# dh's product split between ScalarE and VectorE, with the orders of all stages laid anew

## The chip, the core and the metric

The kernel runs on one core of one Trainium2 chip. The time is device microseconds of one execution, from the core's own start to its end. Five engines run their own queues of instructions in order: TensorE (PE, with PEld for its weight loads), VectorE (DVE), ScalarE (ACT), GpSimd (POOL) and SyncE (SP, which here only issues transfers). An instruction that waits for a semaphore holds up everything behind it in its own queue, and nothing in the others unless they wait for its result.

## The reference

The forward pass is a layer norm, an S4 convolution of length L = 2048 over D = 512 channels with N = 128 states, and a gate from a two-layer network of width 1792. The kernel returns the forward output and the gradients of eleven inputs for a given `grad_out`:

```python
def _A_ref(u, A_re, A_im, B_re, B_im, C_re, C_im, log_dt, Dskip):
    ...
    P = jnp.exp(logdA[:, :, None] * l[None, None, :])
    K = jnp.einsum("dn,dnl,dn->dl", Cc, P, dB).real
    ...                                   # y = irfft(rfft(u padded) * rfft(K padded)), first L
    y = y + u * Dskip[None, None, :]
def _B_ref(x, w1, w2):
    h = jnp.einsum("bsd,df->bsf", x, w1)
    h = _silu(h)
    return jnp.einsum("bsf,fd->bsd", h, w2)
xn = _layernorm(x, axis=-1)
s = _A_ref(xn, ...)
g = _silu(_B_ref(xn, w1, w2))
return x + s * g
# reference(): this output, and jax.vjp(...)(grad_out) for u, A, B, C, log_dt, Dskip, w1, w2
```

All arrays are bf16. The term that the change touches belongs to the backward pass of the network: with DO the gradient at the output of w2, dh = (DO w2^T) * silu'(h), which then gives dw1 = xn^T dh and the part of dx that passes through w1.

## The kernel before

The work is in four stages, which by the trace take about 0 to 146 us (stage 1), 146 to 240 (stage 2), 240 to 399 (stage 3) and 399 to 668 (stage 5).

Stage 1 computes the network forward (ps_h, ps_o) beside the tables of powers for the convolution. The tables end in pairs of products XYg = ex * b_w and ex * b_s (L645), which are stored to DRAM (XYd) and come back in another layout as XYc (L840). Small masks that later stages use (mwk, MK, Sel, nSel, L315 to L345) are made on VectorE near the end.

Stage 2 turns these tables into the kernel K in chunks: ScalarE copies XYc into CY (L876, L877), VectorE multiplies (m, L891), TensorE sums (ps_k), and Kout goes to DRAM. Beside it xn is transposed (XT), goes through the first halves of a Fourier transform by matrix products (FA, FX), and w2 is transposed (w2o). When the last chunk of K is stored (Kud), it is loaded again as K_b, and its spectrum is made in stage 3, which holds the products of the spectra and the inverse transforms.

Stage 5 has two parts. Up to about 528 us come dw2 (ps_w of L1575, w for halves of one 128-row block), the "slabs" that collect the convolution's gradients per state (Gbd L1632, ps_V L1644, its eviction Vb, products T L1656 and L1659, ps_S L1674), YTl, and the first half of dh. From there come dx (ps_dx L1808, followed by the layer norm's backward on VectorE and ScalarE, L1813 to L1832), the rest of dh, dw1 (ps_w L1908, evicted into o10b), the last gradients of the states, and the output rows (zS, L1457 to L1470). dx needs W1 transposed, which seven transfers on SP bring (W1T, L1898, into the same memory KXW that dw2 used); they can start when dw2 is done.

dh is computed in 28 calls of `Bwd.dh(n)`: four chunks of 512 tokens by seven pairs of 128 rows. A call has ScalarE make sd = silu'(h) from hsb (L213), TensorE make eight matmuls into one PSUM tile ps_da (two such buffers, shared with ps_V), and VectorE multiply both into dhT (L1747). Then it issues on SP the load of an h to come and the stores that are pending, and calls `turn(n-1)`: eight transposes of the pair before into PSUM (pt_dh, L1762), an eviction into dhk (two buffers), and a store of dhk to dhd, which the next call issues.

What sets the order is not a scheduler but four strings. `play()` reads a string letter by letter; each letter advances one generator by one step, which issues its instructions on whichever engines it uses. A capital letter lets the step's evictions from PSUM (`ev`, L77) go by VectorE instead of ScalarE. In stage 5: h is one dh, w half a block of dw2, l a step of the slabs (49 in all), y a step of the states' YTl, u a load of w2's transpose, o one W1T load, x half of one dx tile, m one dw1 product, t one load of dh for dw1, f the states' end, z the output, r the rest.

Of the kernel before, what the change touches and what calls it, by code (L numbers as in the profile page):

```python
# [9 lines left out]
ALU = mybir.AluOpType  # L10
# [18 lines left out]
NU = 656  # L29


SCORE_1 = "pppppppppppgpgpgppGppgppppppggpppppgppgppppppppppgpppgpgppppppggppppppgpppppgppMpGGpppgppppgppgpppgpmpppppgppmgppgpppppppppgpgppppppmmmppgpgpmgpgGgttMmGmtmtgggmgGgmmmmgtgGGg"
SCORE_2 = (
    "guuuuuuuTutTKuWtttkkgkgttucgtggttttotguuuTgkttkTcktugtgtTgkottuuu",
    "uuuTTu",
    "tguuuwuwcttgtwUug",
    "uutKTtuggkuwkTTktuutKKKk",
)
SCORE_3 = (
    "TTU",  # L40
    "FFqkFFFfTfTftqqfqffqFFnDffnkffTkufffDfUfffdnudFUF",
    "aaadkadfdafdddfkDdFfafdfafBDvvvAkbnbvbdFadsgakdgaakigsbgdddGddDpaifDjjbiadjaaaxpbxbdevpivxBxvvtjzezxggpgsgstsgxzxzejxizeiztXzizbzqjbiyybsbpbcybsbgbpxssexjxpxpyzxsjxxxszexezczlylesssyszyslzZysZZCCCCCC",
)
SCORE_5 = (
    "uyuwuLLuWWhwyhuwyyLhlylwluyywlhllhllyluw",
    "whYYlwlLhYLwwwLlYyywLwlwlwWHyLlwwlwlLWywlyLylHwWyLllwylhwwolYhlLHlolYolhlolyloooHllLyLLxlhlx",
    "xzxxxxxhxzhhzxxhhxHfHxfxxxHxhxxHhtHthtxtxxzfxhxxMHxttxxttfzfmtffxttMMfftxmtfxtmxtfMtftrfmrffzMmrMfzzfffzzrm",
)


# [43 lines left out]
def drain(k, parts, names):  # L94

    for n in names:
        for _ in parts[n]:
            pass
# [10 lines left out]
def play(kk, score, **parts):  # L109

    for ch in score:
        if ch == " ":
            continue
        kk.by_dve = ch.isupper()
        next(parts[ch.lower()], None)
    kk.by_dve = False
# [95 lines left out]
def DSILU(nc, pool, out, in_):  # L212
    nc.scalar.activation(out=out, in_=in_, func=ACT.Derivative_silu)  # L213
# [531 lines left out]
def stage_1(k):  # L745
# [47 lines left out]
    def power():  # L793
        for _, _, fn, a in sorted(todo, key=lambda x: x[:2]):
            fn(*a)
            yield

    def tables():
        lo.close("bs", "tab", "pr")
        tables_open(k, fs)  # L800
        while True:
            tables_0(k)
            yield

    def forward():
        for _ in gf:
            yield
            settle(k)
    parts = dict(p=power(), m=gm, g=forward(), t=tables())
    i = SCORE_1.index("t")  # L810
    play(k, SCORE_1[:i], **parts)
    drain(k, parts, "pm")
    play(k, SCORE_1[i:], **parts)
    drain(k, parts, "g")
# [892 lines left out]
class Bwd:  # L1707
# [25 lines left out]
    def dh(self, n):  # L1733
        k, nc = self.k, self.k.nc
        tc_, f0 = n // 7, 2 * (n % 7)
        if f0 == 0:
            self.dhT = self.fb.tile([P, FT, 512], BF16, name="dhT", tag="dhT")
        assert k.w2t >= f0 // 2
        hs = self.hs.pop(n)
        sd = self.fw.tile([P, 2, 512], BF16, name="sd", tag="sd")  # L1740
        DSILU(nc, self.fw, sd[:], hs[:])
        ps = k.pd.tile([P, 2, 512], F32, name="ps_da", tag="pd")
        for j in range(2):
            ft = f0 + j
            for dk in range(DK):
                nc.tensor.matmul(out=ps[:, j], lhsT=self.W2T[:, ft // 2, dk, j * P:(j + 1) * P], rhs=self.DOT[tc_][:, dk], start=(dk == 0), stop=(dk == DK - 1))  # L1746
        nc.vector.tensor_tensor(out=self.dhT[:, f0:f0 + 2, :], in0=ps[:], in1=sd[:], op=ALU.mult)  # L1747
        if n + 3 < 28:
            self.ld_h(n + 3, nc.gpsimd if n < 7 else None)
        self.of[n] = self.dhT  # L1750
        self.flush()
        if n:
            self.turn(n - 1)
# [207 lines left out]
```

## Time and profile before

| | |
|---|---|
| median of 3 runs | 665.48 us (665.18 to 667.17) |
| profiled execution | 670.08 us |
| its span, first to last instruction | 668.1 us |
| granted TensorE clock, mean | 0.956 |
| busy: PE / DVE / ACT / POOL | 566.7 / 571.5 / 444.8 / 96.3 us |
| dh product on VectorE | 28 at 1221 ns |

In the profile's rows, a group is line, engine, operation, output and input, shapes and count; then busy time, the mean of one in ns, and after the last bar how long its engine had stood idle before such instructions, and for whom. A row of a stretch has the busy time and count of each engine, then the granted clock of TensorE, the share of the DMA engines that were busy, and GB/s. A row of the timeline has start, duration, engine and line, and in brackets the idle time ahead of it. SPq is the queue that issues transfers; its times are those of issuing, not of the transfer.

### The profile page before, as it was taken

To read this page: it belongs to the slowest core of one execution; us is meant where nothing else is said; L and a number is where in the kernel's file an instruction comes from. 1 tells how busy PE (TensorE), PEld (TensorE's weight loads), DVE (VectorE), ACT (ScalarE), POOL (GpSimd) and SP (SyncE) were. 2 spreads that over 40 slices of the span, in tenths; PEclk is the share of its full clock that TensorE was granted. 3 is DMA by queue.
4 is the path that set the end of the run, shared out by engine and by line. 5 is a ranking of instruction groups with operands and counts; after the bars stand their busy time and mean duration, and the time that the engine had idled before them with its cause. 6 is when DMAs were issued, how large, how long until landed. Compare 5 with 4: busy or idle time off the path is not lost. (4 is left out here: it accounts for less than half of the span.)

```text
span 668.1 us, 14321 instructions
## 1 busy us (share of the span) xinstructions
PE 566.7 (85%) x5668; PEld 341.6 (51%) x5668; DVE 571.5 (86%) x953; ACT 444.8 (67%) x538; POOL 96.3 (14%) x170
## 2 busy tenths in 40 slices
PE   2887897777686977799998779899999799999997
PEld 1333343245565766567775545454555344455553
DVE  7999899989799757998999998787888777889785
ACT  5799999967779725998989815763367345352232
POOL 1120100111002132121223152211111000000000
PEclk9999999898788797999999979999999799999999
DMA  8675777687699769965577889888969947986886
GB/s 257 215 256 183 261 257 262 232 288 209 180 281 318 228 181 269 306 225 168 152 231 211 179 236 248 254 241 198 234 189 207 267 126 215 270 249 218 276 278 199
DMA packets 173623, 154.58 MB, mean 231 GB/s; under 512 B 70575, under 2 KB 141751, under 8 KB 173557
## 3 DMA queue, kind: packets, MB, share of 16 engines
q1 hardware_dynamic: 157428, 112.70, 58.2%
q0 software_dynamic: 11920, 38.08, 18.2%
q10 hardware_dynamic: 4208, 2.89, 1.5%
q8 instruction: 44, 0.72, 0.4%
q14 instruction: 23, 0.18, 0.1%
HBM read 76.81 MB, written 67.65 MB: 216 GB/s over the span
## 5 line engine op out<-in xcount | busy, mean ns | idle before, releaser
L725 PE MATMUL ps_h<-XNT,W 128*128 128x512 bf16 x224 | 55.3, 392 | 18.7 <-ACT hs L77 14.5
L1746 PE MATMUL ps_da<-DOT,W2T 128*128 128x512 bf16 x224 | 53.2, 381 | 0.9 <-DVE dhT L1747 0.9
L698 PE MATMUL ps_o<-W,aT 128*128 128x512 bf16 x224 | 51.9, 379 | 2.0 <-ACT aT L727 2.0
L1808 PE MATMUL ps_dx<-KXW,dhT 128*128 128x512 bf16 x224 | 52.3, 387 | 0.0
L1575 PE MATMUL ps_w<-DO_all,KXW 128*128 128x512 bf16 x224 | 51.4, 379 | 0.0
L1908 PE MATMUL ps_w<-dhc,xn 128*128 128x448 bf16 x256 | 49.4, 352 | 0.0
L725 PEld LDWEIGHTS <-W 128*128 128x128 bf16 x224 | 22.3, 100 | 48.4 <-issue 25.2
L1747 DVE TENSOR_TENSOR dhT<-ps_da,sd 128x1024 bf16<-128x1024 f32 x28 | 34.2, 1221 | 13.5 <-ACT sd L213 11.2
L77 ACT CAST FA<-ps_f 128x1024 bf16<-128x1024 f32 x40 | 39.5, 1035 | 9.0 <-issue 6.2
L173 PE MATMUL ps_s<-FA,Wf 128*64 128x256 bf16 x384 | 36.9, 337 | 10.1 <-ACT FX L77 5.2
L77 ACT CAST FZ<-ps_i 128x1024 bf16<-128x1024 f32 x43 | 43.0, 1078 | 2.8 <-PE ps_i L187 2.8
L77 ACT COPY dhk<-pt_dh 128x1024 bf16<-128x1024 bf16 x18 | 18.2, 1009 | 30.0 <-PE pt_dh L1762 15.1
L1908 PEld LDWEIGHTS <-xn 128*128 128x128 bf16 x256 | 25.0, 98 | 23.7
L1817 ACT ACTIVATE dxn<-dxn,c,rstd 128x512 f32<-128x512 f32 x16 | 13.0, 814 | 35.6 <-DVE c L1816 35.6
L698 PEld LDWEIGHTS <-aT 128*128 128x128 bf16 x224 | 21.8, 98 | 28.7 <-ACT aT L727 2.5
L187 PEld LDWEIGHTS <-Vi 64*128 64x128 bf16 x576 | 27.4, 94 | 16.7 <-issue 6.2
L1808 PEld LDWEIGHTS <-dhT 128*128 128x128 bf16 x224 | 21.7, 99 | 25.3 <-issue 2.2
L1367 PE MATMUL ps_v<-FZ,TI 128*128 128x256 bf16 x192 | 26.2, 292 | 9.8 <-DVE FZ L162 8.7
L1746 PEld LDWEIGHTS <-W2T 128*128 128x128 bf16 x224 | 21.4, 98 | 25.5 <-issue 3.1
L173 PEld LDWEIGHTS <-Wf 128*64 128x64 bf16 x384 | 24.7, 124 | 18.1 <-issue 13.6
L727 ACT ACTIVATE aT<-ps_h 128x1024 bf16<-128x1024 f32 x28 | 31.5, 1130 | 3.1 <-PE ps_h L725 2.9
L1575 PEld LDWEIGHTS <-KXW 128*128 128x128 bf16 x224 | 20.8, 98 | 24.7 <-issue 2.3
(313 smaller groups left out, 1466.7 us busy)
## 6 DMA issues: line engine op xcount, KB each, us to landing
XTd<-XT SPq DMA_DIRECT2D x20, 512.0 KB, 7.0
XP<-UXd POOLq DMA_DIRECT2D x16, 512.0 KB, 5.3
XTl<-XTd SPq DMA_DIRECT2D x31, 256.0 KB, 3.7
hTd<-hs SPq DMA_DIRECT2D x28, 256.0 KB, 3.5
aTd<-aT SPq DMA_DIRECT2D x28, 256.0 KB, 3.2
dhc<-dhd SPq DMA_DIRECT2D x16, 448.0 KB, 5.9
XYd<-XYg SPq DMA_DIRECT2D x25, 256.0 KB, 3.4
hsb<-hTd SPq DMA_DIRECT2D x18, 256.0 KB, 3.7
```

The lines of the kernel that those rows point to most:

```text
L77: (k.nc.vector.tensor_copy if k.by_dve else k.nc.scalar.copy)(out=out, in_=in_)
L173: nc.tensor.matmul(out=ps[64 * h:64 * h + 64, c, j], lhsT=k.Wf[:, c, 0:64], rhs=A[:, 2 * (v + j) + h], start=True, stop=True)
L187: nc.tensor.matmul(out=ps[:, h, j], lhsT=Vc[z], rhs=y[z, c, v % 4 + j, :], start=(n == 0), stop=(n == len(Y) - 1))
L698: nc.tensor.matmul(out=pso[:], lhsT=aT[:, ft, tt * P:(tt + 1) * P], rhs=W2[:, ft, :], start=(ft == 0), stop=(ft == FT - 1))
L725: nc.tensor.matmul(out=ps[:, j], lhsT=W1[:, dk, ft * P:(ft + 1) * P], rhs=XNT[:, dk], start=(dk == 0), stop=(dk == DK - 1))
L727: nc.scalar.activation(out=aT[:, f0:f0 + 2, :], in_=ps[:], func=ACT.Silu)
L1367: k.nc.tensor.matmul(out=ps[:, j], lhsT=k.TI[:, t0 + j, c, :], rhs=Z[:, 2 * (t0 + j) + c], start=(c == 0), stop=(c == 1))
L1575: nc.tensor.matmul(out=ps[:], lhsT=A[:, t, :], rhs=k.DO[:, t, :], start=(t == 0), stop=(t == T - 1))
L1746: nc.tensor.matmul(out=ps[:, j], lhsT=self.W2T[:, ft // 2, dk, j * P:(j + 1) * P], rhs=self.DOT[tc_][:, dk], start=(dk == 0), stop=(dk == ...
L1747: nc.vector.tensor_tensor(out=self.dhT[:, f0:f0 + 2, :], in0=ps[:], in1=sd[:], op=ALU.mult)
L1808: nc.tensor.matmul(out=psx[:], lhsT=dhT[:, ft, t % 4 * P:(t % 4 + 1) * P], rhs=self.W1T[:, ft, :], start=(ft == 0), stop=(ft == FT - 1))
L1908: nc.tensor.matmul(out=ps[:], lhsT=k.xn[:, t, dk * P:(dk + 1) * P], rhs=ch[i][:, t, :], start=(t == 0), stop=(t == T - 1))
```

## The change

The product in `Bwd.dh` becomes two instructions. ScalarE copies ps_da from PSUM into its place in dhT, as bf16; VectorE then multiplies that place by sd in place, with both operands in SBUF.

```diff
             ft = f0 + j
             for dk in range(DK):
                 nc.tensor.matmul(out=ps[:, j], lhsT=self.W2T[:, ft // 2, dk, j * P:(j + 1) * P], rhs=self.DOT[tc_][:, dk], start=(dk == 0), stop=(dk == DK - 1))
-        nc.vector.tensor_tensor(out=self.dhT[:, f0:f0 + 2, :], in0=ps[:], in1=sd[:], op=ALU.mult)
+        d = self.dhT[:, f0:f0 + 2, :]
+        nc.scalar.copy(out=d, in_=ps[:])
+        nc.vector.tensor_tensor(out=d, in0=d, in1=sd[:], op=ALU.mult)
         if n + 3 < 28:
             self.ld_h(n + 3, nc.gpsimd if n < 7 else None)
```

All four strings are replaced as well. Their sequence is another, and so is the choice of capitals; in stage 5 the number of letters of each kind is the same. There, VectorE evicts 15 dhk of 28 (10 before), 9 YTl of 16 (6), 7 o10b of 16 (6), 5 blocks of dw2 of 14 (3) and 10 Vb of 32 (10). In stage 3 the capitals go from 39 to 38. The exponential that makes dtb4 stands between the first and the second string of stage 5; the first string is now 96 letters long (40 before), so it comes later. One line of the table, the second string of stage 5:

```diff
-    "whYYlwlLhYLwwwLlYyywLwlwlwWHyLlwwlwlLWywlyLylHwWyLllwylhwwolYhlLHlolYolhlolyloooHllLyLLxlhlx",
+    "LWwHwYllwlLolYlooohyLlLHooYollhlhl",
```

At the end of stage 1, on VectorE, the masks stood ahead of the last two pairs of XYg:

```order
L343 TENSOR_SCALAR mwk<-mwk 128x1
L344 TENSOR_SCALAR Sel<-mwk 128x32
L343 TENSOR_SCALAR mwk<-mwk 128x1
L344 TENSOR_SCALAR Sel<-mwk 128x32
L345 TENSOR_SCALAR nSel<-Sel 128x128
L645 TENSOR_TENSOR XYg<-ex,b_w 128x8x128
L645 TENSOR_TENSOR XYg<-ex,b_s 128x8x128
L645 TENSOR_TENSOR XYg<-ex,b_w 128x8x128
L645 TENSOR_TENSOR XYg<-ex,b_s 128x8x128
```

Now the last pair stands ahead of the masks from L327 on, and the pair before it further ahead still:

```order
L323 TENSOR_TENSOR mwk<-mwk 128x1
L324 SCALAR_TENSOR_TENSOR mwk<-mwk 128x1
L645 TENSOR_TENSOR XYg<-ex,b_w 128x8x128
L645 TENSOR_TENSOR XYg<-ex,b_s 128x8x128
L327 CAST mwk<-num 128x16
L328 TENSOR_SCALAR mwk<-mwk 128x16
L331 CAST MK<-mwk 128x16x2
L332 TENSOR_SCALAR MK<-mwk 128x16x2
L331 CAST MK<-mwk 128x16x2
```

The last four XYg have moved forward past the masks of L327 to L345.

Early in stage 2, on ScalarE, the second copy into CY (L876, L877) followed this work, where FA and FX belong to the spectrum of xn, XT to its transposes and Kout to the chunks of K:

```order
L546 COPY TF<-pt_tf 128x1024 x4
L77 CAST FA<-ps_f 128x4x64x4 x8
L77 COPY XT<-pt_xt 128x1024 x4
L77 CAST Kout<-ps_k 128x41x16 x2
L77 COPY XT<-pt_xt 128x1024 x2
L77 CAST FX<-ps_s 128x2x512
L876 COPY CY<-XYc 128x128x6
L877 COPY CY<-XYc 128x512x2
```

Now it comes behind one Kout and two XT, with a block of w2o between:

```order
L546 COPY TF<-pt_tf 128x1024 x4
L77 CAST FA<-ps_f 128x4x64x4 x8
L77 COPY XT<-pt_xt 128x1024
L77 COPY w2o<-pt_w_1799 128x1024
L77 CAST Kout<-ps_k 128x41x16
L77 COPY XT<-pt_xt 128x1024
L876 COPY CY<-XYc 128x128x6
L877 COPY CY<-XYc 128x512x2
```

Four XT, one Kout and one FX have moved behind the copy.

At the end of stage 5's first part, on SP, the W1T loads (DMA_TRANSPOSE) stood between loads for the slabs (XTl), loads of h (hsb) and stores of dhk; this is from the second of the seven on:

```order
L1898 DMA_TRANSPOSE KXW<-in_B_w_dram 128x2x512
L1621 DMA XTl_5911<-XTd 64x2048
L1898 DMA_TRANSPOSE KXW<-in_B_w_dram 128x2x512
L1731 DMA hsb<-hTd 128x1024
L1794 DMA dhd<-dhk 512x1x256
L1621 DMA XTl_5912<-XTd 64x2048
L1898 DMA_TRANSPOSE KXW<-in_B_w_dram 128x2x512
L1621 DMA XTl_5913<-XTd 64x2048
L1898 DMA_TRANSPOSE KXW<-in_B_w_dram 128x2x512 x3
L1731 DMA hsb<-hTd 128x1024
L1794 DMA dhd<-dhk 512x1x128 x2
L1731 DMA hsb<-hTd 128x1024
```

Now, from one row ahead of the first of the seven on:

```order
L1621 DMA XTl_5912<-XTd 64x2048
L1900 DMA_TRANSPOSE KXW<-in_B_w_dram 128x2x512
L1621 DMA XTl_5913<-XTd 64x2048
L1900 DMA_TRANSPOSE KXW<-in_B_w_dram 128x2x512 x3
L1731 DMA hsb<-hTd 128x1024
L1796 DMA dhd<-dhk 512x1x192
L1796 DMA dhd<-dhk 512x1x64
L1731 DMA hsb<-hTd 128x1024
L1796 DMA dhd<-dhk 512x1x256
L1900 DMA_TRANSPOSE KXW<-in_B_w_dram 128x2x512 x3
L1731 DMA hsb<-hTd 128x1024
L1796 DMA dhd<-dhk 512x1x128 x2
```

The last XTl load now stands between the first and the second transpose, and the other six transposes come in two groups of three.

Since the change adds two lines to `dh`, all lines behind it have numbers greater by two (L1898 is L1900, L1794 is L1796).

More of the change, by code (lines that the diff above doesn't have):

```diff
@@ L29 @@
 NU = 656
-SCORE_1 = "pppppppppppgpgpgppGppgppppppggpppppgppgppppppppppgpppgpgppppppggppppppgpppppgppMpGGpppgppppgppgpppgpmpppppgppmgppgpppppppppgpgppppppmmmppgpgpmgpgGgttMmGmtmtgggmgGgmmmmgtgGGg"
+SCORE_1 = "ppppppppppppgppggGpppppgppppggppppppgpppppggpppppppgpppppppppgggpppgppppgpppppGMppGpppgpppppgppppggppppppgpppgpmppppppppgpgppppppgmpmppgmpgpmpggmGMmmgtmtmmGggtmggGggtgmtGmGg"
 SCORE_2 = (
[L34 to L37, printed above, removed]
+    "ugTuuTuuuuuTtugTwKgktcTtggttkgttukuuouTtttkttcgt",
+    "gtgkktggkttTuouTuuuuuutugwuugtuUKtttcwgkuguugwukttkut",
+    "tTuWu",
+    "TtKkKk",
 )
 SCORE_3 = (
-    "TTU",
-    "FFqkFFFfTfTftqqfqffqFFnDffnkffTkufffDfUfffdnudFUF",
-    "aaadkadfdafdddfkDdFfafdfafBDvvvAkbnbvbdFadsgakdgaakigsbgdddGddDpaifDjjbiadjaaaxpbxbdevpivxBxvvtjzezxggpgsgstsgxzxzejxizeiztXzizbzqjbiyybsbpbcybsbgbpxssexjxpxpyzxsjxxxszexezczlylesssyszyslzZysZZCCCCCC",
+    "TT",
+    "UFFFFFffkfqqqtqtfffqFkftFFnfDnfkTffffDfffdkudUuFUF",
+    "aadaadadffdddnFnkdDffafaidffBDvbvAvbvaddgsbakgkaagbdFgdddsGdkdDpajjiDibadaabaxbiedxtvfvvppBvsxzjtgsxgsxziegpggxezxzxjzjzezzXbibtziijyybbspespbybcbbxxssxxppqgyzjxlxxxzsexcezjzsyeslysszzsssYzlyZZCCCCCC",
 )
 SCORE_5 = (
-    "uyuwuLLuWWhwyhuwyyLhlylwluyywlhllhllyluw",
-    "whYYlwlLhYLwwwLlYyywLwlwlwWHyLlwwlwlLWywlyLylHwWyLllwylhwwolYhlLHlolYolhlolyloooHllLyLLxlhlx",
-    "xzxxxxxhxzhhzxxhhxHfHxfxxxHxhxxHhtHthtxtxxzfxhxxMHxttxxttfzfmtffxttMMfftxmtfxtmxtfMtftrfmrffzMmrMfzzfffzzrm",
+    "uwuuuuWhWywLwyWyylYLhYwylywlwhwlwylllhuLlluHllYLWHyLylywlwllwylhWlllyHYwLwLwlwLwlLYHwYlLylwhlyLW",
+    "LWwHwYllwlLolYlooohyLlLHooYollhlhl",
+    "xzxxxxxxxzHxHzhxHxhxHffhxxxxxHhxxfHHttHtthxxxfzhxMxHxxftttxfftfftmMttxMtxxfftfxtxMMztmffMrtzMffzzfrrffmrtmmzz",
 )
```

## The prediction

> **What bounds the kernel now.** I read the page's first part for the engines, then the busy time by stretches for where each engine is full, then the groups of instructions for prices, and the timeline at the two places where the new orders differ most. The profiled execution took 670.08 us: its span is 668.1, so 1.98 lie around it, and it stands 4.6 above the median of 665.48. I sum against 670.08 and subtract the differences from the median.
>
> ```profile
> span 668.1 us, 14321 instructions
> PE 566.7 (85%) x5668; PEld 341.6 (51%) x5668; DVE 571.5 (86%) x953; ACT 444.8 (67%) x538; POOL 96.3 (14%) x170
> ...
> core 0: us, PE busy (x) PEld busy (x) DVE busy (x) ACT busy (x) POOL busy (x), PEclk, DMA share, GB/s
> ...
> 200.00:300.00 100.00, 79.68 (x1283) 62.67 (x1281) 81.47 (x114) 73.32 (x80) 24.36 (x47) 0.90 0.85 254
> 300.00:400.00 100.00, 85.39 (x1054) 64.47 (x1049) 96.07 (x80) 78.20 (x84) 27.49 (x42) 0.97 0.70 195
> 400.00:440.00 40.00, 36.40 (x355) 19.84 (x353) 33.28 (x56) 27.27 (x30) 8.89 (x15) 1.00 0.94 254
> 440.00:480.00 40.00, 38.84 (x383) 20.16 (x381) 31.80 (x49) 15.63 (x19) 8.37 (x15) 1.00 0.89 220
> 480.00:520.00 40.00, 38.69 (x449) 22.40 (x445) 34.66 (x52) 27.47 (x30) 5.56 (x11) 1.00 0.86 209
> ...
> 600.00:640.00 40.00, 40.00 (x215) 20.19 (x214) 33.82 (x65) 11.64 (x22) 0.00 (x0) 1.00 0.79 267
> ```
>
> VectorE is full in stage 3 (96.07 of 100), but dh's product does not run there. It runs from 413 to 605, where TensorE is the fuller engine in every stretch: 36.40, 38.84 and 38.69 of 40, then 40.00. So what VectorE gives up there can return no more than the time in which TensorE stands still for it, and from 600 on there is none.
>
> **The split itself.** These are the groups of stage 5 that it touches:
>
> ```profile
> L1746 PE MATMUL ps_da<-DOT,W2T 128*128 128x512 bf16 x224 | 53.2, 381 | 0.9 <-DVE dhT L1747 0.9
> L1747 DVE TENSOR_TENSOR dhT<-ps_da,sd 128x1024 bf16<-128x1024 f32 x28 | 34.2, 1221 | 13.5 <-ACT sd L213 11.2 <-PE ps_da L1746 2.2
> L213 ACT ACTIVATE sd<-hsb 128x1024 bf16<-128x1024 bf16 x28 | 29.3, 1056 | 0.0
> L77 ACT CAST Vb<-ps_V 128x1024 bf16<-128x1024 f32 x22 | 22.2, 1014 | 11.0 <-PE ps_V L1644 5.7 <-issue 5.1
> L77 ACT COPY dhk<-pt_dh 128x1024 bf16<-128x1024 bf16 x18 | 18.2, 1009 | 30.0 <-PE pt_dh L1762 15.1 <-DMA dhd<-dhk 14.2 <-ACT sd L213 0.6
> L1762 PE MATMUL pt_dh<-ident_bfloat,dhT 128*128 128x128 bf16 x224 | 17.1, 219 | 0.7 <-DVE dhT L1747 0.6
> L77 DVE COPY dhk<-pt_dh 128x1024 bf16<-128x1024 bf16 x10 | 6.8, 683 | 3.0 <-DMA dhd<-dhk 3.0
> L1469 DVE TENSOR_TENSOR zS<-zS,zg 128x1024 bf16<-128x1024 bf16 x8 | 5.5, 684 | 4.1 <-DMA zg<-gd 4.1
> ```
>
> VectorE loses 28 products of 1.221 us that read PSUM and gets 28 all-bf16 ones. The nearest row is zS at 684 ns, the same size and types in SBUF: 28 x (1.221 - 0.684) = 15.0 us less. ScalarE gets 28 casts of PSUM to bf16 at 128x1024. The nearest is Vb at 1.014: 28.4 us more. One dh's chain from TensorE's last matmul to the finished dhT grows from 1.22 to 1.01 + 0.68 = 1.70, and crosses two queues. Nothing waits for that at once: the transposes of a pair are issued only after the next pair's eight matmuls (53.2 / 28 = 1.90 us).
>
> The new order spends half of the relief: in stage 5 eleven more evictions go by VectorE (five dhk, three YTl, two KXW, one o10b). At 0.683, the dhk row, that is 7.5 us, so VectorE keeps a net relief of 7.5 us over 265. For ScalarE the eight large ones return 8 x 1.009 = 8.1; with the three small ones, which I bound between 0 and the same 1.009 each, its net is +17 to +20 us. The stretch with the most ScalarE work in this stage, 480 to 520, has 27.47 of 40 and six products: 27.5 + 6.1 = 33.6. It stays off the bound, so I cost the casts at nothing; their cover is 12 us of ScalarE's idle time per 40, and without it each would cost up to 1.0.
>
> The page "VectorE: DVE Perf Modes" of the Trainium skill, section "Rules for kernel authors", speaks against this change: for an elementwise operation on a matmul's output it says to accept the slow rate, or to copy to SBUF first where many operations follow. Here one follows. By that rule the split only adds engine time, 28 x (1.01 + 0.68 - 1.22) = 13 us; the trace agrees on the sum, but those 13 us lie on an engine that idles.
>
> **Stages 1 and 2.** At the end of stage 1 the last two pairs of table products (XYg) move ahead of the masks of L327 to L345; in stage 2 the second CY copy moves forward in ScalarE's queue. The timeline of VectorE and then of ScalarE:
>
> ```profile
> 127.73 0.17 DVE L327 CAST mwk<-num 128x16 f32<-128x16 int32 x1
> ...
> 130.73 1.22 DVE L645 TENSOR_TENSOR XYg<-ex,b_w 128x1024 bf16<-128x1024 f32 x1
> ...
> 134.14 1.22 DVE L645 TENSOR_TENSOR XYg<-ex,b_s 128x1024 bf16<-128x1024 f32 x1
> ...
> 144.94 1.83 DVE L891 TENSOR_TENSOR m<-CY 128x1536 bf16<-128x1536 bf16 x2 [2.29 <-ACT CY L877]
> ```
>
> ```profile
> 130.32 1.13 ACT L631 ACTIVATE b_w<-b_w,halfpi 128x1024 f32<-128x1024 f32 x1
> ...
> 143.05 0.85 ACT L876 COPY CY<-XYc 128x768 bf16<-128x768 bf16 x1 [4.92 <-DMA XYc<-XYd]
> ```
>
> The masks fill 127.73 to 130.73, 3.0 us, ahead of the last four XYg. VectorE later stands 2.29 us for CY, which waits for the load of what these XYg store. Moving the masks behind them could bring the store 3.0 us forward, but the last XYg pair still needs b_w, ready at 131.45. It could then end at 131.45 + 2 x 1.14 = 133.7, not 135.4: at most 1.6. I take half, -0.75 (range 0 to -1.6).
>
> ```profile
> 168.53 0.71 ACT L77 CAST Kout<-ps_k 128x656 bf16<-128x656 f32 x1 [4.27 <-PE ps_k L945]
> ...
> 172.25 0.87 ACT L876 COPY CY<-XYc 128x768 bf16<-128x768 bf16 x1
> ```
>
> ```profile
> 174.17 2.70 DVE L891 TENSOR_TENSOR m<-CY 128x1536 bf16<-128x1536 bf16 x3 [4.50 <-ACT CY L877]
> ```
>
> ScalarE stood 4.27 us for the second Kout's matmuls with the CY copy queued behind, and VectorE 4.50 for CY. In the new order the copy comes after one Kout and two XT, not two Kout, six XT and an FX; five instructions and that wait no longer stand ahead, so the 4.50 can go whole. What is late next is the kernel's way from K to its spectrum, by the waits of 230 to 282 (total, count, longest):
>
> ```profile
> POOL K_b L997 <- DMA K_b<-Kud: 6.7, 1, 6.7
> ...
> ACT FA L77 <- issue: 6.2, 1, 6.2
> ```
>
> These waits between 230 and 282 follow the last K chunk, and their instructions are not shortened. What VectorE wins at 174 reaches the end only if the chunks come sooner. Between 0 and -4.5 I take -2. Stage 3 is VectorE's own: its evictions by VectorE go from 39 to 38 letters (one F and one Y more, two T and one Z fewer), the rest is the same work in another sequence: 0, range -2 to +2.
>
> **Stage 5 up to dx (399 to 528).** TensorE idles 3.60 + 1.16 + 1.31 = 6.1 us in the three stretches to 520, and most at the end, by the timeline:
>
> ```profile
> 519.17 6.16 SPq L1898 DMA_TRANSPOSE KXW<-in_B_w_dram  x3
> ...
> 522.16 0.69 DVE L77 COPY dhk<-pt_dh 128x1024 bf16<-128x1024 bf16 x1 [2.68 <-DMA dhd<-dhk]
> ...
> 523.84 0.78 PE L1644 MATMUL ps_V<-XTl,Gbd 128*32 128x256 bf16 x16 [3.09 <-DVE Gbd L1632]
> ...
> 527.91 3.17 PE L1808 MATMUL ps_dx<-KXW,dhT 128*128 128x512 bf16 x7
> ```
>
> In the chain that ended last, in order of time:
>
> ```profile
> 514.12 7.95 DMA dhd<-dhk
> ```
>
> And the stretches of 4 us, with the granted clock behind POOL's column:
>
> ```profile
> 520.00:524.00 4.00, 0.91 (x20) 0.61 (x16) 1.84 (x4) 3.03 (x4) 0.00 (x0) 1.00 1.20 258
> 524.00:528.00 4.00, 3.31 (x41) 1.59 (x38) 3.59 (x5) 0.00 (x0) 0.00 (x0) 0.58 1.09 246
> 528.00:532.00 4.00, 4.00 (x11) 1.44 (x12) 3.65 (x4) 0.00 (x0) 0.00 (x0) 0.57 0.99 268
> ```
>
> The dhk store issued at 514.12 took 7.95 us among the W1 transposes; VectorE stood for it, behind it Gbd, behind that TensorE: 3.09 + 0.69 idle in 520 to 528, and then 8 us at a granted clock of 0.57, worth 8 x 0.43 = 3.4. So the place costs about 7.2. The new order takes the XTl loads out from between the transposes and issues these as 1, 3 and 3. Two dhk stores stand between the two threes, and two after them. I think the stall gets smaller, because more dhk evictions leave VectorE's queue free for Gbd, but the store still goes out amid transposes. Between all of it gone (-7.2) and the slower case below (+8.4) I take -2; and of the 6.1 before it, where waits for VectorE are few, -0.5.
>
> The clock's recovery is a rule of "TensorE: Matmul & The Clock Gate", Part 1, of the Trainium skill: half rate after an idle window of some 3.4 us, full again after as long a busy one. By it the slow stretch would cost 3.4 x 0.5 = 1.7 and the place 5.5. The trace shows more than 8 us between 0.57 and 0.58, and I keep its 7.2.
>
> **Stage 5 from dx on.** TensorE is busy 40.00 of 40 at 600; a dh needs 1.90 + 17.1 / 28 = 2.51 us of it, ScalarE 1.06 + 1.01 and every other time 1.0 of dhk: 2.57 on average. Nearly even, so runs of four dh's could lag by under 1 us, which the dx between make up. I take 0, range -1 to +1.5; the last transfers, of the same kind and number, 0, range -1 to +1.
>
> **Sum.** -0.75 - 2 + 0 - 2.5 + 0 + 0 = -5.25: the profiled 670.08 becomes 664.8, and the median 660.2. I say 660.5.
>
> **Rivals.** (a) No net change, about 665.5: the 4.5 of stage 2 ends in the unchanged way from K, and stage 5 finds the same stall in another queue. For it speaks that TensorE leads all through stage 5; against it that two named stalls have their cause moved. (b) Larger gain, about 655: stage 2's 4.5, stage 1's 0.75 and most of the 7.2 (say 5.5) go, 10.75 in all. For it: VectorE's relief falls just where the chain ran over dhk and Gbd. Against: the dhk store's 7.95 is the DMA's. (c) Slower, about 671: the transposes as two threes. From the start of a three at 519.17 to dx at 527.91 went 8.74 us. After the last three the new order has four slab steps (about 0.85 each: 41.8 us of L1644 and L1674, over 49 letters) and two dh's, 8.4 us of TensorE work. If that work itself stands behind a dhk store caught among the transposes, TensorE idles 5 us more than now and the slow clock lasts 8 us longer: 5 + 3.4 = 8.4; less the 2.75 of stages 1 and 2, +5.65, or 671.1. It decides from where a dhk store issued behind the first three lands more than 8.4 us later. The rows behind the 41.8:
>
> ```profile
> L1644 PE MATMUL ps_V<-XTl,Gbd 128*32 128x256 bf16 x512 | 22.0, 290 | 5.6 <-DVE Gbd L1632 3.1 <-ACT Vb L77 1.8 <-DVE dhT L1747 0.6
> L1674 PE MATMUL ps_S<-T,Sel 128*32 128x512 bf16 x96 | 13.4, 394 | 1.9 <-DVE T L1659 1.0 <-DVE T L1656 0.7
> L1674 PE MATMUL ps_S<-T,nSel 128*32 128x512 bf16 x32 | 6.4, 395 | 0.0
> ```
>
> **Chances.** A measurement tells about 0.3%, 2.0 us, from no change. The forecast (657 to 663.4) 0.42, (b) 0.12: faster 0.54. (a) 0.14. (c) and other losses in orders that I could only read 0.32. The range 651 to 672 leaves out the far end of (b), under a tenth, and the far end of the losses, about a tenth. Those that win alone: 654 to 663.4.
>
> **What the profile after would show.** Right: the product at about 0.68, the casts near 1.01, VectorE's wait at the second CY under 1 us, TensorE's idle time before dx under 3.8, a shorter stretch at 0.57. Wrong: a TensorE wait of over 5 us just before ps_dx, ScalarE over 36 of 40 anywhere in stage 5 with TensorE waiting for dhT, or the span of stages 2 and 3 longer than now (146 to 399).

## The result: 1.6% slower, lost in stage 3

The changed kernel took 676.0 us (median of 4, 675.1 to 679.1) against 666.3 for the kernel before (median of 4, 665.2 to 667.2): a ratio of 1.0159, interval 1.0119 to 1.0198. Here and below, a ratio leaves out executions more than 1.5% above the fastest of their kernel. Its profiled execution took 675.44 us with a span of 673.6, 5.5 more than the 668.1 before. The profile of before is of an execution 3.8 above this median of 666.3, so the two profiles account for 5.5 of the 9.7 us between the medians; where the rest lies they do not show. The page's first part and the stretches of the changed kernel, with the columns as in the prediction:

```profile
span 673.6 us, 14323 instructions
PE 562.5 (84%) x5668; PEld 338.5 (50%) x5668; DVE 563.5 (84%) x962; ACT 462.8 (69%) x557; POOL 95.7 (14%) x170
...
200.00:300.00 100.00, 78.42 (x1305) 60.92 (x1304) 81.43 (x100) 76.38 (x84) 23.89 (x46) 0.97 0.82 245
300.00:400.00 100.00, 75.37 (x936) 56.33 (x935) 82.35 (x70) 72.43 (x78) 23.73 (x36) 0.90 0.73 171
...
440.00:480.00 40.00, 35.12 (x410) 20.36 (x408) 32.64 (x53) 26.78 (x30) 9.99 (x18) 0.98 1.09 217
480.00:520.00 40.00, 39.19 (x390) 20.67 (x389) 35.96 (x57) 21.46 (x26) 6.62 (x13) 0.98 0.96 240
```

One row stands out: 300 to 400, where VectorE had been busy 96.07 of 100 and is now busy 82.35. The stages can be cut at four marks, read from the first and last starts of a tile's instructions:

| mark | before | changed | difference of the piece |
|---|---|---|---|
| last group of ps_k (K is complete) | 238.8 | 231.7 | -7.1 |
| last group of ps_v (end of stage 3) | 398.7 | 405.4 | +13.8 |
| first ps_dx | 527.9 | 535.8 | +1.2 |
| end of the span | 668.1 | 673.6 | -2.4 |

So stages 1 and 2 won 7.1 us, stage 5 won 1.2, and stage 3 lost 13.8 (a piece is the time between two marks).

**Where stage 3 lost it.** The timeline of the changed kernel, VectorE and TensorE first:

```profile
384.09 1.23 DVE L125 TENSOR_TENSOR cm_t<-XP,KXW 128x2048 bf16<-128x2048 bf16 x1 [9.93 <-DMA XP<-DXd]
...
391.60 0.69 DVE L1434 TENSOR_TENSOR cG<-cG,co 128x1024 bf16<-128x1024 bf16 x1 [3.02 <-DMA cG<-in_grad_out_dram]
```

```profile
386.63 0.40 PE L187 MATMUL ps_i<-XP,Vi 64*128 64x256 bf16 x2 [10.12 <-DVE XP L126]
```

VectorE stood 9.93 us for a load of XP, then 3.02 for one of cG; TensorE stood behind it for 10.12. With another 0.80 for XP at 371.07, VectorE's waits for loads come to 13.75 us, the size of the loss. The XP loads are the last two from DXd, on POOL's queue, and beside them SP's queue brings the first inputs of dw2 by transposing loads (L1568, from aTd into KXW):

```profile
364.82 0.76 POOL L1425 DMA_DIRECT2D cG<-in_grad_out_dram  x1 [6.10 <-DVE cm_t L125]
365.57 1.09 POOL L1358 DMA_DIRECT2D XP<-DXd  x2
```

```profile
365.88 4.97 SPq L1568 DMA_TRANSPOSE KXW<-aTd  x1
372.46 1.27 SPq L91 DMA_DIRECT2D Sd<-S_s  x2
373.83 12.79 SPq L1568 DMA_TRANSPOSE KXW<-aTd  x1
```

```profile
L1358 POOL DMA_DIRECT2D XP<-DXd x8: 530/530/549, 301.7 to 366.1; - x8
...
DMA to landing us min/median/max: 3.6/4.8/17.9
```

Both XP loads stood behind the cG load, were issued together at 365.6 and 366.1, and 0.3 us after the first a transposing load was issued on SP. The first XP load landed in 5.4 us, the second in 17.9, and the co and cG loads behind it on POOL's queue took 18.1 and 17.1. Before, the two went out one by one, and none took over 6.9:

```profile
360.81 0.55 POOL L1358 DMA_DIRECT2D XP<-DXd  x1 [1.43 <-PE ps_i L187]
...
370.17 0.55 POOL L1358 DMA_DIRECT2D XP<-DXd  x1
```

```profile
363.76 3.06 SPq L1568 DMA_TRANSPOSE KXW<-aTd  x1
...
372.15 3.28 SPq L1568 DMA_TRANSPOSE KXW<-aTd  x1
```

```profile
DMA to landing us min/median/max: 3.8/4.9/6.9
```

While they ran together, the DMA engines were more than full by the sum of their packets' times (share, then GB/s, in the last two columns; the changed kernel):

```profile
366.00:372.00 6.00, 3.61 (x49) 2.93 (x48) 5.20 (x3) 4.57 (x6) 1.41 (x3) 1.00 0.99 209
372.00:378.00 6.00, 3.15 (x43) 2.17 (x40) 2.12 (x3) 4.22 (x5) 0.76 (x1) 1.00 1.30 99
378.00:384.00 6.00, 0.00 (x0) 0.00 (x0) 0.00 (x0) 0.00 (x0) 0.00 (x0) 0.59 1.42 131
```

From 372 to 378 they moved only 99 GB/s at a share of 1.30, and from 378 to 384 no engine computed at all. From the first transposing load on, the sequence of these loads and of the Sd stores on SP is the same in both kernels, and so is that of the cG and co loads on POOL. Only the place of the two XP loads among them moved.

### The profile page after: what moved, and what is told of

Same layout as the page of the kernel before. It is cut to its first block, busy times and chain, and to the rows that moved or that the text cites. A ratio compares the mean times of both kernels' runs of the same rounds, so it can differ in the third digit from the quotient of the medians.

```text
span 673.6 us, 14323 instructions
## 1 busy us (share of the span) xinstructions
PE 562.5 (84%) x5668; PEld 338.5 (50%) x5668; DVE 563.5 (84%) x962; ACT 462.8 (69%) x557; POOL 95.7 (14%) x170
## 5 line engine op out<-in xcount | busy, mean ns | idle before, releaser
L725 PE MATMUL ps_h<-XNT,W 128*128 128x512 bf16 x224 | 57.6, 405 | 15.8 <-ACT hs L77 10.2
L698 PE MATMUL ps_o<-W,aT 128*128 128x512 bf16 x224 | 54.1, 390 | 2.5 <-ACT aT L727 2.5
L1810 PE MATMUL ps_dx<-KXW,dhT 128*128 128x512 bf16 x224 | 50.5, 379 | 0.0
L187 PE MATMUL ps_i<-XP,Vi 64*128 64x256 bf16 x256 | 30.4, 279 | 17.5 <-DVE XP L126 13.7
L173 PE MATMUL ps_s<-FA,Wf 128*64 128x256 bf16 x384 | 34.9, 315 | 11.6 <-DVE FA L162 3.6
L1748 ACT CAST dhT<-ps_da 128x1024 bf16<-128x1024 f32 x28 | 28.2, 1006 | 9.2 <-PE ps_da L1746 8.9
L77 ACT COPY XT<-pt_xt 128x1024 bf16<-128x1024 bf16 (+1 forms) x31 | 28.1, 951 | 7.3 <-PE pt_xt L1019 6.0
```

The costliest lines, as they stand in the source:

```text
L77: (k.nc.vector.tensor_copy if k.by_dve else k.nc.scalar.copy)(out=out, in_=in_)
L173: nc.tensor.matmul(out=ps[64 * h:64 * h + 64, c, j], lhsT=k.Wf[:, c, 0:64], rhs=A[:, 2 * (v + j) + h], start=True, stop=True)
L187: nc.tensor.matmul(out=ps[:, h, j], lhsT=Vc[z], rhs=y[z, c, v % 4 + j, :], start=(n == 0), stop=(n == len(Y) - 1))
L698: nc.tensor.matmul(out=pso[:], lhsT=aT[:, ft, tt * P:(tt + 1) * P], rhs=W2[:, ft, :], start=(ft == 0), stop=(ft == FT - 1))
L725: nc.tensor.matmul(out=ps[:, j], lhsT=W1[:, dk, ft * P:(ft + 1) * P], rhs=XNT[:, dk], start=(dk == 0), stop=(dk == DK - 1))
L1748: nc.scalar.copy(out=d, in_=ps[:])
```

## The experiments

The theory after the result: the 10 us are a collision of the transposing load with the two XP loads, and without it the changed kernel is faster than before. A first rival: the XP loads are simply issued too late, behind cG. A second: the split itself costs, by ScalarE's queue. Letters of stage 3's last string: j is one XP load from DXd, y one piece of output with its next co and cG loads, l one transposing load for dw2; the diffs show only the part of the string that changes. Executions of one kernel spread over some 10 us on the chips of these runs (before: 664 to 676), so times are given as ratios to the kernel before on the same chip.

**Two transposing loads later.**

```diff
-yzjxlxxxzsexcezjzsyeslysszzsssYzlyZZCCCCCC"
+yzjxlxxxzsexcezjzsyesysszzsssYzlyZlZCCCCCC"
```

> The changed kernel, with two of the three early transposing loads for dw2 (L1568) moved one store of Sd later each in SP's queue at the end of stage 3. Theory (collision): in the changed kernel the last XP load (issued 366.1, landed 384.1) is slow because these transposing loads run through it; without them VectorE's wait of 9.93 us for XP falls under 1 us, the stage's end comes 8 to 13 us earlier, and the time is 663 to 668 instead of 676. Rival (late issue): the load is late because it stands behind a cG load in POOL's queue and two of them are issued together; then the wait stays near 10 us and the time at 674 to 677.

Ratio 0.9903 (0.9867 to 0.9939), or 0.994 by the medians of all executions (666.3 against 670.6); span 660.6, stage 3 ends at 392.9. The XP loads are issued at the same time as in the changed kernel, and as a pair, but now land in 4.4 and 6.6 us (no XP load of the kernel took over 7.4), and VectorE waits for none of them (POOL's and SP's timeline, and the XP tile's row):

```profile
366.24 1.09 POOL L1358 DMA_DIRECT2D XP<-DXd  x2
```

```profile
375.45 3.53 SPq L1568 DMA_TRANSPOSE KXW<-aTd  x1
```

```profile
DMA to landing us min/median/max: 3.8/4.8/7.4
```

That refutes the first rival: late issue alone costs nothing here.

**The two XP loads earlier.**

```diff
-ppqgyzjxlxxxzsexcezjzsyesl
+ppqjgjyzxlxxxzsexcezzsyesl
```

> The changed kernel, with the last two XP loads moved ahead of the last-but-one pair of cG and co loads in POOL's queue, transposing loads as they are. Both the collision theory and the late-issue rival expect the XP loads to be issued at about 357 to 362, ahead of the transposing load of 366, and the wait of 9.93 us to go: 663 to 668. They differ in what is left: by the collision, the co and cG loads, which still meet the transposing loads, stay slow (17 to 18 us to landing; VectorE's 3.0 us for cG stays); by late issue they land in about 4 us.

Ratio 0.9947 (0.9900 to 0.9994), span 662.9, stage 3 ends at 393.9. The loads go out at 358.5 and land in at most 7.2 us. The expectation about the rest missed: the cG and co loads that still meet the transposing loads of 366.5 and 374.4 land in 4.7 to 6.6 us, not in 17 to 18. So the transposing load does not slow every transfer that it meets.

**Which transposing load, and how many XP loads.** Three kernels, with one execution of each, so that their landing times say more than their spans: only the second transposing load later, only the third later, and only the first of the two XP loads earlier.

```diff
-zsyeslysszzsssYzlyZZCCCCCC"
+zsyesyslszzsssYzlyZZCCCCCC"     # second later
+zsyeslysszzsssYzyZZlCCCCCC"     # third later
-ppqgyzjxlxxxzsexcezjzsyesl
+ppqjgyzxlxxxzsexcezjzsyesl     # one XP load earlier
```

> The changed kernel with only the second of the three early transposing loads one store of Sd later, the third in its place. If it is the second one (issued 365.9, together with the two XP loads) that slows XP, VectorE's wait for XP is under 1.5 us and the span 660 to 664. If it takes the third one in the same stretch (issued 373.8), the wait stays over 5 us and the span over 667.

> The changed kernel with only the third of the three early transposing loads one store of Sd later; the second one still meets the two XP loads at about 366. If the second alone makes the collision: VectorE's wait for XP stays over 5 us, stage 3 ends after 400. If it takes the second and the third in one stretch: the wait is under 2 us and stage 3 ends at 393 to 396.

> The changed kernel with only the first of the last two XP loads moved ahead of the last-but-one cG and co pair in POOL's queue: the transposing load of 366 meets one XP load instead of two. If the pair is needed: the XP load lands in under 8 us and VectorE waits under 2 us for it, stage 3 ends at 393 to 397. If one is enough: it lands in over 12 us, the wait is over 4 us.

With the second one later the span is 663.3, stage 3 ends at 395.3, and XP lands in at most 6.8 us. With only the third later nothing is mended, span 675.7, stage 3 to 404.9, and one XP load takes 19.0 us; the XP pair at 366.46 meets the second at 366.77:

```profile
366.77 5.08 SPq L1568 DMA_TRANSPOSE KXW<-aTd  x1
...
392.76 2.03 SPq L1568 DMA_TRANSPOSE KXW<-aTd  x1
```

```profile
386.10 1.23 DVE L125 TENSOR_TENSOR cm_t<-XP,KXW 128x2048 bf16<-128x2048 bf16 x1 [10.95 <-DMA XP<-DXd]
```

With one XP load moved away the span is 665.2 and stage 3 ends at 393.9, though the other is still in flight when the second transposing load is issued; it landed in 4.2 us (the row's 7.6 is another load):

```profile
365.29 0.55 POOL L1358 DMA_DIRECT2D XP<-DXd  x1
```

```profile
367.27 3.60 SPq L1568 DMA_TRANSPOSE KXW<-aTd  x1
```

```profile
DMA to landing us min/median/max: 3.8/4.6/7.6
```

So the collision is of the pair of 512 KB loads with the second transposing load, and moving any one of them ends it. The last of these kernels changes two things at once, though: one load instead of two, and 2.0 us from the load to the transposing load instead of 0.3, as far as in the kernel before (370.17 and 372.15). Whether the number of loads or their closeness counts was not tested. The third transposing load is not needed, and its 12.79 us of issuing in the changed kernel were a result, not a cause.

**The changed kernel once more,** to see whether the collision is a chance of one execution.

> The changed kernel as it is, on the chip of the next three runs. Collision theory: VectorE waits 8 to 12 us for the last XP load again (landing over 14 us), stage 3 ends near 405, the time is 1.003 to 1.016 of before. If the wait is only a chance of one execution, it is absent here and stage 3 ends near 393.

Ratio 1.0113 (1.0040 to 1.0187). It is there again: landing up to 19.8 us, a wait of 11.67, stage 3 ends at 406.4, span 676.6. All eight executions of the changed kernel, in both sets, took 675 us or more.

**The split alone, and the new orders without it.**

```diff
 # split_only: the kernel before with
-        nc.vector.tensor_tensor(out=self.dhT[:, f0:f0 + 2, :], in0=ps[:], in1=sd[:], op=ALU.mult)
+        d = self.dhT[:, f0:f0 + 2, :]
+        nc.scalar.copy(out=d, in_=ps[:])
+        nc.vector.tensor_tensor(out=d, in0=d, in1=sd[:], op=ALU.mult)
 # after_fused, x1_fused: the reverse in the changed kernel and in x1_l_late
```

> The kernel before, with the product of dh split and nothing else changed. Theory (TensorE leads stage 5): the product falls from 1.22 to 0.68 us, ScalarE gains 28 casts near 1.01, and the time stays within 2 us of before: 664 to 668. Rival (the casts hold up ScalarE's queue, and dhk, Vb and sd behind them): 669 or more, with ScalarE's idle time before dhT's cast over 10 us in all and TensorE waiting for Vb or dhT. A gain of over 3 us would say that VectorE led stage 5 after all.

> The changed kernel, with the product of dh in one instruction as before, the orders as changed. Theory (the loss is the order of stage 3): 675 to 679, since the new order of stage 5 counts on the relief: eleven more evictions on VectorE and 15 us more of products. Rival (the split is what costs): under 673.

> x1_l_late with dh's product in one instruction again. Stage 3 ends near 393 as there. Theory (the new order of stage 5 uses up VectorE's relief): stage 5 lasts 2 to 5 us longer than the 267.7 of x1_l_late, 0.993 to 0.998 of before in time. Rival (TensorE leads, the split is worth nothing in either order): 266.5 to 269, 0.988 to 0.992 of before.

The split alone: ratio 1.0021 (0.9980 to 1.0063), no change that can be told. (Its stages 1 to 3 have the order of before, and its stage 3 took 157.5 us, near the 159.9 of before.) Its two instructions, by the groups of stage 5:

```profile
L1748 ACT CAST dhT<-ps_da 128x1024 bf16<-128x1024 f32 x28 | 28.3, 1009 | 13.2 <-PE ps_da L1746 13.2
L1749 DVE TENSOR_TENSOR dhT<-dhT,sd 128x1024 bf16<-128x1024 bf16 x28 | 19.3, 689 | 25.4 <-ACT dhT L1748 25.4
```

ScalarE did stand 13.2 us for TensorE before the casts, and VectorE 25.4 for the casts, and neither showed in the time. The new orders without the split: 1.0031 (0.9994 to 1.0067), less than the expected 675 to 679 would be as a ratio (1.013 to 1.019). Its interval overlaps that of the changed kernel's second set (1.0040 to 1.0187), and lies below that of the first (1.0119 to 1.0198). Its one profile, of its slowest execution, has the collision too (landing up to 19.0 us, a wait of 11.0, stage 3 to 405.8), but three of its ten executions took only 667.5 to 669.2, and no trace shows what they did. The split runs in stage 5 alone, so it is not in the 13.8 us; whether it costs something beside them in the order that collides stays open. The mended kernel without the split: 0.9917 (0.9879 to 0.9954), the same as with it (0.9903); by the medians of all executions 0.996 and 0.994. The rival in its expectation, that the split is worth nothing in either order, fits where nothing collides: stage 5 lasted 264.3 us, under the 266.5 to 269 that the rival expected, and not more than the 267.7 with the split.

**Stage 5 as before, stages 1 to 3 mended.** The edit puts back stage 5's three strings and the fused product in x1_l_late.

> x1_l_late with stage 5 as before the change (its strings, and the product in one instruction). Theory (stages 1 to 3 bring nearly all of the gain): stage 3 ends near 393, stage 5 lasts 268 to 271, the span is 661 to 664, the time 0.990 to 0.995 of before. Rival (stage 5's split and order bring a good part): the span is 665 or more.

Span 661.7, stage 3 ends at 395.3, stage 5 lasts 266.4; ratio 0.9970 (0.9928 to 1.0012), which misses the expected 0.990 to 0.995, as stage 5 misses its 268 to 271. By the profile nearly all of the gain is in stages 1 to 3; by the times some of it may be in stage 5, and the intervals overlap. That stays open.

**Both mends, and the first one again.** x12 has the edits of the first two experiments together; x1_again is x1_l_late unchanged.

> Both mends at once: the two XP loads early and the two transposing loads late. No collision is left in either; stage 3 ends at 392 to 395, the time is 0.987 to 0.993 of before, as x1_l_late. If the cG and co loads still met the transposing loads in x1_l_late to a cost, it is up to 0.3% better than that.

> x1_l_late once more beside x12, on one chip: 0.987 to 0.994 of before, stage 3 ends at 392 to 395, stage 5 lasts 266 to 269.

Both mends: 0.9961 (0.9932 to 0.9991), span 664.2, not better than one, and short of the expected 0.987 to 0.993. x1_l_late again: 0.9924 (0.9885 to 0.9963), so it is faster than before in both sets, by under 1%, and, with x1_fused, the best that was run. Its second profile is slower, span 667.5 with stage 3 to 400.2 (392 to 395 expected), and shows that the mend is not complete: a cG load of 256 KB, issued at 375.79, 0.07 us behind a transposing load, took 9.7 us, and VectorE waited for it.

```profile
385.59 0.69 DVE L1434 TENSOR_TENSOR cG<-cG,co 128x1024 bf16<-128x1024 bf16 x1 [5.70 <-DMA cG<-in_grad_out_dram]
```

## Why the prediction was wrong

The sign was wrong, and the step that failed is the sentence on stage 3: "the rest is the same work in another sequence: 0, range -2 to +2". It measured +13.8: VectorE stood 10.7 us for XP and 3.0 for cG. That step counted evictions on the engines that compute and never looked at what the new sequence does to the transfers: on POOL, where two loads had come to stand together behind a waiting one, and on SP beside it. The order of POOL's queue, which was there to be read, shows the move; it does not show the price, for which no row of before had a pair of 512 KB loads against a transposing load. With that one collision taken out the span was 660.6 and 667.5 in two profiles, -7.5 and -0.6 against before, and the ratios 0.9903 and 0.9924 put the median of 666.3 at 660 and 661, or at 662 by the first one's medians. The forecast of 660.5 was thus near the time of a kernel without the collision, which is not the kernel that was asked about. That it comes so near is in part luck: in the first of these two profiles stages 1 and 2 gave -6.6 (-2.75 was forecast), stage 3 +0.8 (0), stage 5 up to dx +2.7 (-2.5) and from dx on -4.4 (0).

Step by step:

- **The split itself.** Right. The product took 690 ns (684 forecast), the cast 1006 (1014), and the whole is worth nothing by itself, as "I cost the casts at nothing" said. The groups of the changed kernel:

```profile
L1748 ACT CAST dhT<-ps_da 128x1024 bf16<-128x1024 f32 x28 | 28.2, 1006 | 9.2 <-PE ps_da L1746 8.9
L1749 DVE TENSOR_TENSOR dhT<-dhT,sd 128x1024 bf16<-128x1024 bf16 x28 | 19.3, 690 | 12.2 <-ACT dhT L1748 12.0
```

  The page "VectorE: DVE Perf Modes" of the Trainium skill, section "Rules for kernel authors", keeps the copy to SBUF for the case of many operations behind it; here there is one, and that split_only came out at 1.0021 agrees, in that the copy bought nothing.

- **End of stage 1, -0.75.** Too high by 0.66. The side of the load came as forecast: the XYg pair stood 1.49 us for b_w, the bound that the prediction named, ended at 134.2 instead of 135.4, and the CY copy began at 142.15 instead of 143.05. But the masks now stand behind the pair in VectorE's queue, and VectorE reached the first product with CY only at 144.85, with no wait; before it was 144.94 after 2.29. What the prediction left out is that the moved masks fill the time that VectorE had stood idle.

- **Stage 2, -2.** The mechanism was right and the size was too small: the second CY product began at 169.50 with no wait (174.17 after 4.50 before), the fourth at 210.99 (216.24), and K was complete 7.1 us sooner. The prediction took less than half of the 4.50 because it held the way from K to its spectrum for the limit; that way starts with K's last chunk, which came sooner too. The rows of both items, VectorE then ScalarE:

```profile
131.86 1.23 DVE L645 TENSOR_TENSOR XYg<-ex,b_w 128x1024 bf16<-128x1024 f32 x1 [1.49 <-ACT b_w L631]
...
134.14 0.79 DVE L327 CAST mwk<-num 128x16 f32<-128x16 int32 x1
...
144.85 3.56 DVE L891 TENSOR_TENSOR m<-CY 128x1536 bf16<-128x1536 bf16 x4
...
169.50 3.57 DVE L891 TENSOR_TENSOR m<-CY 128x1536 bf16<-128x1536 bf16 x4
```

```profile
142.15 0.84 ACT L876 COPY CY<-XYc 128x768 bf16<-128x768 bf16 x1 [2.20 <-DMA XYc<-XYd]
...
165.51 0.84 ACT L876 COPY CY<-XYc 128x768 bf16<-128x768 bf16 x1 [0.83 <-DMA XYc<-XYd]
```

- **Stage 5 up to dx, -2.5.** Measured +1.2. The stall of 520 to 532 did go: TensorE is busy 10.8 of 12 there and its clock is 1.00.

```profile
520.00:524.00 4.00, 3.37 (x60) 2.36 (x58) 3.95 (x5) 3.73 (x5) 0.00 (x0) 1.00 1.12 240
524.00:528.00 4.00, 3.73 (x52) 2.49 (x55) 3.92 (x7) 2.72 (x4) 0.00 (x0) 1.00 1.12 200
528.00:532.00 4.00, 3.71 (x53) 2.59 (x46) 1.51 (x3) 3.76 (x5) 0.00 (x0) 1.00 0.99 212
```

  But the idle time only changed its place. Up to dx TensorE idled 129.00 - 119.16 = 9.8 us before (first row) and 130.20 - 120.16 = 10.0 now (second); what waits now is ps_V for a load of XTl (2.8 us), pt_yt for Y (2.0) and ps_da for evictions of Vb (2.7).

```profile
398.90:527.90 129.00, 119.16 (x1233) 65.00 (x1230) 106.22 (x165) 73.39 (x82) 22.82 (x41) 0.99 0.91 231
```

```profile
405.60:535.80 130.20, 120.16 (x1258) 66.63 (x1256) 108.48 (x178) 80.53 (x89) 22.80 (x41) 0.99 1.01 226
```

```profile
PE ps_V L1644 <- DMA XTl<-XTd: 2.8, 1, 2.8
...
PE pt_yt L1054 <- DVE Y L892: 2.0, 2, 1.0
PE ps_da L1746 <- DVE Vb L77: 1.8, 2, 0.9
...
PE ps_da L1746 <- ACT Vb L77: 0.9, 2, 0.6
```

- **Stage 5 from dx on, 0.** Measured -2.4; 1.7 of it (4 us x 0.43) answers to the slow clock of 528 to 532 before, which is gone. Over all runs that share one order stage 5 lasted 267 to 271 us, so neither number is far from that spread.

- **Rival (c), slower at 671.** Its side was right and its place was wrong. The transposes that it feared, W1's, came in two groups of three and did not hold up dx (TensorE had no idle time just ahead of ps_dx); the ones that did harm were dw2's, some 150 us earlier, and it was not a store of dhk that they caught but the pair of XP loads. The sentence on what would make the forecast wrong, stages 2 and 3 longer than 146 to 399, is the one that came true: 146 to 405.

## What to carry to other kernels

When an order is laid anew, read the queues of the transfers as closely as those of the engines: for each load list what stands ahead of it, with what it is now issued together, and which transfers run beside it. A stage with the least slack (here VectorE at 96 of 100) is where a late load costs most: here 13.75 us of waits became 13.8 us of the stage. And where an engine other than the bound is relieved, as VectorE was in stage 5, price the relief at nothing until a row shows the bound waiting for it: 15 us less of products here moved the time by nothing that could be told.

## What the runs showed of the hardware

Two loads of 512 KB were issued 0.5 us apart on POOL's queue, with a transposing load issued on SP between them, in four profiles: the changed kernel's two, t3_late's and after_fused's. In each the first load landed in 5.4 to 5.6 us and the second in 17.9 to 19.8, and the co and cG loads issued behind it took 12.7 to 20.0. Where one of the three was moved, the two loads took 4.2 to 7.2. From 372 to 384 the DMA engines of these four profiles counted as more than full (1.09 to 1.42) while moving 61 to 131 GB/s (t3_late, from 372 to 378):

```profile
372.00:378.00 6.00, 4.05 (x51) 2.93 (x48) 3.05 (x3) 4.81 (x5) 0.76 (x1) 1.00 1.20 91
```

One 512 KB load issued 2.0 us ahead of such a transposing load took 4.2 (one_j_early) and 4.6 (before); no run has a single one closer. The page "DMA: Bandwidth & Descriptors" of the Trainium skill, section "Queues, rings and completion order", says that a DMA engine takes packets from its queues in turn. By that alone, an estimate from this case's rows: two loads and a transposing load of the same size are 1.5 MB, at the 209 GB/s of 366 to 372 some 7.5 us, and the trace shows more than twice that. What makes the rest was not found out.
